# A planned instruction order: a short linger in TensorE's quarter form, and two constants of the order

## The chip, the cores and the metric

The kernel runs on one core of one Trainium2 chip. The metric is the device time of one execution in microseconds (us); lower is better. A core has TensorE (matmuls, results in eight banks of PSUM), VectorE (DVE in the profile), ScalarE (ACT), GpSimd (POOL) and SyncE (SP, which here only issues DMAs). Only VectorE and ScalarE copy results out of PSUM in this kernel.

## What is computed

Attention for 8 batches, 12 heads, 448 positions and 64 features a head, in which the heads are mixed before and after the softmax, and behind it a feed-forward layer on 3584 rows of 768:

```python
scores = scale * np.matmul(q, k.transpose(0, 1, 3, 2))
scores = np.einsum('bhij,hg->bgij', scores, w_pre)
scores = scores - np.max(scores, axis=-1, keepdims=True)
attn = np.exp(scores)
attn = attn / (np.sum(attn, axis=-1, keepdims=True) + 1e-09)
attn = np.einsum('bhij,hg->bgij', attn, w_post)
attn_out = np.matmul(attn, v)
x = attn_out.transpose(0, 2, 1, 3).reshape(B * S, H * D)
h = np.maximum(x @ w_in, 0.0)
out = h * h @ w_out
```

The matmuls work on bf16 data and sum in f32.

## The kernel before

**The work.** A batch is cut into 45 chunks of up to ten query positions by 12 heads (`chunk`, up to 120 rows and four rows of zeros), 360 chunks in all. Per batch and pair of heads, `score` multiplies q and k (L741) into a bank, and VectorE or ScalarE copies the bank to `snat` (`copy`, L534 and L536). `relayout` moves parts of `snat` by DMAs on SP's queue (L772) into one of 14 buffers `sch`, where the rows of a chunk are positions by heads. The mix of the heads is a matmul with `wmix`: for single chunks L901, for two chunks together `mix_two` (L847). Then follow the row minimum on VectorE (L912, the mix has the sign turned round), the exponential on ScalarE (L915), the reciprocal of the sums on VectorE (L922), the scaled weights `wq` on GpSimd (L925), four matmuls that turn the chunk and mix the heads again (L932), their copy to `atb`, and per half of a batch the product with v (`av`, L978). The feed-forward layer works in units of 128 or 256 rows (`unit`): L1037 multiplies by w_in, VectorE or ScalarE takes the positive part (L1051, L1055), GpSimd squares it (L1058), L1076 multiplies by w_out, and the result goes out through `osb`. These units fill the time in which the chunks leave TensorE free.

**Quarter form.** In the batches 1 to 7, most score groups and all of `mix_two` come as four 64x64 matmuls, each in a quarter of the TensorE array (`mode=BOTH` in the code, 3). This text calls such four a quarter group; one group fills two banks. `av` works in halves by columns (`COLS`), some scores of batch 0 in halves by rows (`ROWS`), all else on the whole array (mode 0, full form).

**The order.** All instructions are ordered in advance by a list scheduler in Python (`Planner`), and the engines then run their lists in order. An operation has a duration per engine (`engs`, ns), a delay until its result counts (`lat`), a priority (`pri`, in chunks; lower goes first), what it waits for, the PSUM banks that it takes (`bank`, a key whose first letter is the kind: m mixes, a turned chunks, g scores and others, f feed-forward) and the bank that it gives back (`frees`). `run` keeps a heap of ready operations for each engine, a list of free banks (`free`) and the room left for each kind (`room`, from `MOST`), and steps from event to event of its own clock. When TensorE is idle in that clock, it takes from the heap the first operation that `fits` (enough free banks and enough room), with these rules:

- If the operation is of another mode than the last one, it is set aside as `first`, and one of the same mode is looked for whose priority is at most `STAY[mode]` behind (2 chunks by rows, 6 by columns, 8 in quarter form; from full form there is no such rule).
- From another mode into quarter form it goes only if at least `TOGETHER` = 2 quarter groups would fit (`company`), or one is overdue (`due`).
- A change of mode is given 95 ns (`TURN`).
- An operation that doesn't fit is put into `kept`, and TensorE takes what fits, so it may leave quarter form for a full matmul while a quarter group waits for banks.

**Priorities and reserves that the change touches.** `score` and `relayout` subtract `AHEAD` (7.4 chunks) from the place of the chunk that they are for. From batch 2 on, `x_piece` turns k and q by DMA transposes on SP's queue (L673, L679). These need the heads side by side, which three "near copies" each of k and q on GpSimd make (`pair_k`, `pair_q`, L660, 640 ns in the order, of the lowest priority of all). The near copies wait in the order until `NEAR_LATE` = 3000 ns after the load of their data and after the previous transpose are done (`late`). This reserve is in the order alone; on the chip a copy waits for what it reads and for its turn in GpSimd's list.

Of the kernel before, what the change touches and what calls it, by code (L numbers as in the profile page):

```python
# [40 lines left out]
PIECE = NPAIR // 2  # L41
NE = 6
NSCH = 14
AHEAD = 7.4
FIFO = 50
IDLE_NS, IDLE_COLS, IDLE_FROM, IDLE_END, IDLE_LOW = 112, 256, 1300, 130000, 0.62
SPELL, PHASE, DROP, RISE = 3413, 1700, 0.4, 0.8
ROWS, COLS, BOTH = 1, 2, 3
PAIR_FROM, PAIRS, PAIR_MORE = 1, 1, 30
UP, ZERO_AT = 4, 4  # L50
TOGETHER, MIX_DUE, SCORE_DUE = 2, 1.5, 1.0
TURN = 95
LATER = 2
ONSET, ONSET_IDLE, ONSET_FROM = 2500, 2500, 20000
NEAR_LAST = 2e6
NEAR_LATE, NEAR_LATE_FROM = 3000, 2
OSTEP = 2
GS, ONE = [(0, 1, 2)], [(0,), (1,), (2,)]
STAY = {ROWS: 2, COLS: 6, BOTH: 8}
# [69 lines left out]
class Planner:  # L129
# [8 lines left out]
    def add(self, eng, ns, pri, fn, deps=(), lat=60, bank=None, frees=None, mode=0):  # L138
        op = Op(eng if isinstance(eng, dict) else {eng: ns}, lat, pri, fn, list(deps), bank, frees, mode)
        self.ops.append(op)  # L140
        return op
# [6 lines left out]
    def run(self):  # L148
        order, events, n = [], [], 0
        ready, busy, held = {}, {}, {}  # L150
        free, room = list(self.banks), dict(self.most)
# [13 lines left out]
        def fits(op):  # L165
            if not op.bank:
                return True
            kind, size = op.bank[0][0], len(op.bank)
            return len(free) >= size and room[kind] >= size and (room["mix"] >= size or kind == "f")

        t, mode, clock, front, turning = 0, 0, Clock(), -100, 0

        def company(heap):
            f, left, got = len(free), dict(room), 0
            for _, _, op in sorted(item for item in heap if item[2].mode == BOTH and item[2].eng is None):
                kind, size = op.bank[0][0], len(op.bank)
                if f >= size and left[kind] >= size and left["mix"] >= size:
                    f -= size
                    left[kind] -= size
                    left["mix"] -= size  # L180
                    got += 1
            return got
        queues = {"LOAD": Queue(), "DMA": Queue()}

        def settle():
# [13 lines left out]
        while True:  # L199
            for eng, heap in ready.items():  # L200
                if eng in queues:
                    x = queues[eng]
# [8 lines left out]
                    while x.op is None and heap:  # L211
                        op = heapq.heappop(heap)[2]
# [17 lines left out]
                if busy[eng] > t:  # L230
                    continue
                kept, short, first = [], False, None
                alone = eng == "PE" and mode != BOTH and company(heap) < TOGETHER
                while heap:
                    item = heapq.heappop(heap)
                    op = item[2]
# [17 lines left out]
                    if first is not None:  # L254
                        if op.mode != mode or op.pri > first[0] + STAY[mode]:
                            kept.append(item)
                            if op.pri > first[0] + STAY[mode]:
                                op, item = first[2], first
# [5 lines left out]
                else:  # L264
                    item = None
                    if first is not None:
                        kept.remove(first)
                        item, op, args = first, first[2], []
                if item is None and eng == "PE" and free and IDLE_FROM <= t < IDLE_END and (
                    t < 9000 or clock.at(t) > 1 or clock.share(t - SPELL, t) < IDLE_LOW  # L270
                ):
                    op = Op({"PE": 0}, 0, 0, self.still, [], None, None, mode)
                    op.eng, op.ns, op.at = "PE", IDLE_NS * clock.at(t), t
                    clock.spells.append((t, t + op.ns))
                    order.append((op, [free[0], mode]))
                    busy[eng] = t + op.ns
                    heapq.heappush(events, (t + op.ns, n, None))
                    n += 1
                if item is not None:
                    for key in op.bank:  # L280
                        held[key] = free.pop(0)
                        room[key[0]] -= 1
                        room["mix"] -= key[0] != "f"
                        args.append(held[key])
                    if len(op.engs) > 1:
                        args.append(eng)
                    op.eng, op.ns, op.at = eng, op.engs[eng], t
                    turning += op.turns
                    if op.front is not None:
                        front = op.front  # L290
                    if eng == "PE":
                        op.ns = (op.ns + TURN * (op.mode != mode)) * clock.at(t)
                        clock.spells.append((t, t + op.ns))
                        mode = op.mode
                    order.append((op, args))
                    busy[eng] = t + op.ns
                    heapq.heappush(events, (t + op.ns, n, None))
                    heapq.heappush(events, (t + op.ns + op.lat, n + 1, op))
                    n += 2
# [4 lines left out]
            t = events[0][0]  # L304
            while events and events[0][0] == t:
                op = heapq.heappop(events)[2]
                if op is None:
                    continue
                if isinstance(op, tuple) and isinstance(op[0], Queue):
                    x, turn_ = op  # L310
# [30 lines left out]
def kernel(  # L341
# [46 lines left out]
    def load_q(b, h0, h1):  # L388
        nc.gpsimd.dma_start(
            out=qs[:, h0:h1, :, :].rearrange("p h r d -> p h (r d)"),  # L390
            in_=q[b, h0:h1, 0:TAIL].rearrange("h (p r) d -> p h (r d)", r=NJ),
        )
# [6 lines left out]
    def load_kv(dst, src, b, h0, h1):  # L399
        nc.gpsimd.dma_start(  # L400
            out=dst[:, h0:h1, :, :].rearrange("p h r d -> p h (r d)"),
            in_=src[b, h0:h1].rearrange("h (p r) d -> p h (r d)", r=NB),
        )
# [143 lines left out]
    def load(rows, each, pri, fn, deps):  # L547
        if len(loads) >= 7:
            deps = list(deps) + [loads[-7]]
        op = add("POOL", 830, pri, fn, deps, lat=850)  # L550
        done = pl.moved("LOAD", rows, each[0], each[1], 0, [op], 1500)
        loads.append(done)
        return done
# [158 lines left out]
    def place_of(b, c):  # L712
        return b * NCHUNK + (ORDER0.index(c) if b == 0 else c)
# [6 lines left out]
    def is_direct(b, c):  # L720
        return b == 0 and C0[1] <= c <= C0[2]
# [5 lines left out]
    def score(b, r, group):  # L727
# [17 lines left out]
        first = min(place_of(b, c) for c in range(C0[r], (C0 + [NCHUNK])[r + 1]) if not is_direct(b, c)) - b * NCHUNK  # L745
        pri = b * NCHUNK + first - AHEAD - 0.6 - (0.7 if r == 0 else 1.4) * (NPAIR - p)
        n = b * (NJ + 1) + r - 2
# [30 lines left out]
    def relayout(b, c):  # L778
# [6 lines left out]
        deps = list(scopy[b, r]) + (list(scopy[b, r - 1]) if r == 1 and cc == 0 else [])  # L785
        pri = n - AHEAD
        if r == 2 and cc == 0:
# [15 lines left out]
        else:  # L803
            o = cc - 1
            if b >= PAIR_FROM:
                pri = n - o % (2 * PAIRS) + 0.1 * (o % (2 * PAIRS)) - AHEAD
            o, step = (2 * CI * (o // 2) + o % 2, 2) if b >= PAIR_FROM else (o, CPR)
# [324 lines left out]
    def gate(step):  # L1132
        return [wq_op[step]] if step in wq_op else []
# [62 lines left out]
    def load_tails(b, n, deps):  # L1196
        tails = [load(24, (24, 32), n, lambda x=x: load_tail(b, x), deps) for x in range(2)]
        tail_in[b] = add("TAIL", 0, n, lambda: None, tails, lat=1000 if b else 0)

    def load_ahead(b, n, g0):  # L1200
        wars = [op for p in range(g0 // 2, g0 // 2 + 3) for op in got_op[b - 1, p]]
        got = [
            load(48, (36, 52), n + LATER, lambda: load_q(b, g0, g0 + 6), wars + gate(n)),
            load(42, (46, 58), n + LATER, lambda: load_kv(ks, k, b, g0, g0 + 6), wars + gate(n)),
        ]
        if g0 == 0:
            load_tails(b, n + LATER, got_tail[b - 1] + gate(n))
        later[b, g0] = add("BOTH", 0, n, lambda: None, got, lat=0)
# [133 lines left out]
```

## Time and profile before

| what | value |
|---|---|
| median of 3 runs | 570.41 us (570.14 to 570.57) |
| the profiled execution | 569.92 us |
| its span, first to last instruction | 567.8 us |
| granted TensorE clock, mean | 1.0 |
| instructions | 17932 |
| quarter matmuls of `score`, L741 (64x64) | 504, mean 361 ns each |
| quarter matmuls of `mix_two`, L847 | 504, mean 363 ns each |
| copies to `snat`, VectorE / ScalarE | 150 of 613 ns / 168 of 551 ns |

The profile is one execution, taken by the hardware profiler. PE is TensorE's matmuls, PEld its weight loads, which overlap them. Matmuls are pipelined, so that the mean of one is longer than the distance to the next; the price of work on TensorE is read from the starts. "The chain of work that ended last" is followed back from the last instruction, at each step to what released it. "The waits" list idle time of an engine and what ended it. "The timeline" lists instructions by start, with like ones in a row merged: start, length, engine, line, operation, what is written and read, shapes, and a count behind an x.

### The profile page before, as it was taken

The page shows a single profiled execution, that of the slowest core. Times are in us where ns is not written, and L with a number is a line of the kernel's source. Part 1 is how long each engine was busy: PE and PEld are TensorE (multiplying, and loading weights), DVE is VectorE, ACT ScalarE, POOL GpSimd, SP SyncE. Part 2 cuts the span into 40 slices and gives each one's busy share as a digit, 9 for nine tenths or more (in the row PEclk, how much of TensorE's full clock was granted, in tenths as well). Part 3 has the DMA queues.
Part 4 walks back from the last instruction along what each step waited for, and adds up shares of the span by engine and source line. Part 5 has one row for each costly group of instructions (what it writes and reads, how often), then busy time and mean ns, then how long its engine had stood idle before and what let it go on. Part 6 is the DMA issues. An engine that isn't in the chain of part 4 may idle for free.

```text
span 567.8 us, 17932 instructions
## 1 busy us (share of the span) xinstructions
PE 559.7 (99%) x6323; PEld 396.5 (70%) x6323; DVE 496.8 (87%) x1108; ACT 447.9 (79%) x1187; POOL 363.7 (64%) x677
## 2 busy tenths in 40 slices
PE   8999999999999999999999999999999999999997
PEld 5668676686676667667677677767768676777785
DVE  7999999999999998999898988989899898898442
ACT  5788989888878888878998899888998988888100
POOL 8776358786685549856778358956777553745351
PEclk9999999999999999999999999999999999999999
DMA  9999849974999749974797649974798756441011
GB/s 137 211 178 217 165 117 181 208 135 103 151 203 153 175 97 181 176 162 101 136 198 161 161 104 162 195 145 128 131 192 164 134 142 108 111 99 58 1 57 55
DMA packets 129949, 80.85 MB, mean 142 GB/s; under 512 B 59274, under 2 KB 126588, under 8 KB 129860
## 3 DMA queue, kind: packets, MB, share of 16 engines
q1 hardware_dynamic: 80756, 46.29, 37.2%
q0 software_dynamic: 49104, 33.43, 36.3%
q8 instruction: 49, 0.80, 0.6%
q14 instruction: 40, 0.33, 0.1%
HBM read 45.61 MB, written 11.01 MB: 100 GB/s over the span
## 4 chain that ended last, share of the span: by engine, by line
PE 86%; DVE 5%; ACT 3%; issue 2%; POOL 2%; DMA 1%; DVEq 0%; ACTq 0%; POOLq 0%
PE bank L1076 25%; PE bank L1037 24%; PE bank L932 13%; PE bank L978 6%; PE bank L741 6%; PE bank L847 5%; PE bank L901 3%; DVE mn L912 2%; ACT es L915 2%; PE bank L907 1%; DMA sch<-snat 1%; PE bank L1301 1%; DVE atb L534 1%; PE bank L596 1%; POOL wq L925 1%
## 5 line engine op out<-in xcount | busy, mean ns | idle before, releaser
L915 ACT ACTIVATE es<-bank,mn 124x448 bf16<-124x448 f32 (+1 forms) x360 | 228.3, 643 | 34.3 <-DVE mn L912 30.0
L912 DVE TENSOR_REDUCE mn<-bank 124x1 f32<-124x448 f32 (+1 forms) x360 | 208.9, 612 | 6.8 <-PE bank L847 5.5
L1076 PE MATMUL bank<-w,h 128*128 128x384 bf16 (+2 forms) x912 | 180.2, 324 | 0.2 <-DVE hr L1051 0.2
L1037 PE MATMUL bank<-xt,w 128*128 128x256 bf16 (+1 forms) x1632 | 164.5, 254 | 0.7 <-ACT es L915 0.2
L1037 PEld LDWEIGHTS <-w 128*128 128x128 bf16 x1632 | 133.7, 98 | 25.3 <-issue 10.9
L1058 POOL TENSOR_TENSOR h<-hr 128x512 bf16<-128x512 f32 x112 | 115.9, 1038 | 40.3 <-DVE hr L1051 21.4
L925 POOL TENSOR_SCALAR wq<-wback_two,rc 124x120 bf16<-124x120 f32 x252 | 88.8, 363 | 72.0 <-DVE rc L922 49.2
L932 PEld LDWEIGHTS <-es 124*112 124x112 bf16 (+2 forms) x1440 | 107.0, 130 | 29.7 <-issue 4.9
L534 DVE CAST atb<-bank 112x480 bf16<-112x480 f32 (+3 forms) x196 | 118.1, 614 | 10.1 <-PE bank L932 8.9
L932 PE MATMUL bank<-wq,es 124*112 124x120 bf16 (+2 forms) x1440 | 119.1, 218 | 1.1 <-POOL wq L925 0.4
L1076 PEld LDWEIGHTS <-h 128*128 128x128 bf16 x912 | 79.6, 98 | 56.6 <-issue 18.1
L536 ACT CAST atb<-bank 112x480 bf16<-112x480 f32 (+3 forms) x187 | 99.2, 542 | 17.8 <-PE bank L932 16.6
L534 DVE CAST snat<-bank 128x448 bf16<-128x448 f32 x150 | 89.4, 613 | 3.3 <-PE bank L741 2.4
L536 ACT CAST snat<-bank 128x448 bf16<-128x448 f32 x168 | 85.0, 551 | 7.6 <-PE bank L741 6.8
L915 ACT ACTIVATION_READ_ACCUMULATOR es<-bank,mn 124x1 f32 (+1 forms) x360 | 75.3, 209 | 0.0
L1051 DVE TENSOR_SCALAR hr<-bank 128x512 f32<-128x512 f32 x76 | 52.2, 688 | 19.4 <-PE bank L1037 16.5
L925 POOL TENSOR_SCALAR wq<-wback,rc 124x120 bf16<-124x120 f32 (+1 forms) x94 | 33.4, 364 | 38.7 <-DVE rc L922 27.5
L741 PE MATMUL bank<-kt,qz 64*64 64x448 bf16 (+1 forms) x528 | 45.8, 361 | 0.7 <-ACT qz L536 0.6
L1100 POOL DMA_DIRECT2D out_dram<-osb x33 | 19.8, 600 | 35.5 <-DVE osb L534 18.1
L847 PE MATMUL bank<-sch,wmix 64*64 64x448 bf16 x504 | 42.4, 363 | 0.1
L978 PE MATMUL bank<-atb,vs 112*64 112x192 bf16 (+3 forms) x864 | 40.4, 250 | 0.0
L978 PEld LDWEIGHTS <-vs 112*64 112x64 bf16 x864 | 36.4, 110 | 3.9 <-issue 3.2
(80 smaller groups left out, 399.4 us busy)
## 6 DMA issues: line engine op xcount, KB each, us to landing
sch<-snat SPq DMA_DIRECT2D x318, 105.0 KB
out_dram<-osb POOLq DMA_DIRECT2D x21, 384.0 KB, 3.7
vs<-in_v_dram POOLq DMA_DIRECT2D x16, 336.0 KB, 7.4
ks<-in_k_dram POOLq DMA_DIRECT2D x14, 336.0 KB, 7.7
qs<-in_q_dram POOLq DMA_DIRECT2D x14, 288.0 KB, 7.1
w<-in_moe_w_in_dram POOLq DMA_DIRECT2D x6, 512.0 KB, 14.2
w<-in_moe_w_out_dram POOLq DMA_DIRECT2D x4, 768.0 KB, 20.6
out_dram<-osb POOLq DMA_DIRECT2D x8, 192.0 KB, 3.9
```

The source lines that it names most:

```text
L534: nc.vector.tensor_copy(out=out_, in_=in_)
L536: nc.scalar.copy(out=out_, in_=in_)
L741: nc.tensor.matmul(slot[m0:m1, 0:S], lhsT=lhsT[:, m0:m1], rhs=kt[i][half, :, at_, :], start=True, stop=True,)
L847: nc.tensor.matmul(got[i + x][o0:o1, 0:S], lhsT=w[k0:k1, c0:c0 + o1 - o0], rhs=srcs[i + y][k0:k1, :], start=True, stop=True,)
L912: nc.vector.tensor_reduce(out=mn[i][0:rows, :], in_=slots[mk][0:rows, 0:S], axis=AX.X, op=ALU.min)
L915: nc.scalar.activation(out=es[i][0:rows, 0:S], in_=slots[mk][0:rows, 0:S], func=ACT.Exp, scale=-1.0, bias=mn[i][0:rows, 0:1], accum_out=sm ...
L925: nc.gpsimd.tensor_scalar(out=wq[i][0:rows, :, 0:ns], in0=back[0:rows, :, 0:ns], scalar1=rc[i // 2][0:rows, i % 2:i % 2 + 1], scalar2=1.0, ...
L932: nc.tensor.matmul(slot[0:P_KEYS, jb * H * ns:(jb + 1) * H * ns], lhsT=es[i][0:rows, jb * P_KEYS:(jb + 1) * P_KEYS], rhs=wq[i][0:rows, :, ...
L978: nc.tensor.matmul(v_[64 * hh:64 * hh + 64, i, 0:x1 - x0], lhsT=vs[:, 2 * c2 + hh, jb, :], rhs=atb[half][:, jb, 2 * c2 + hh, x0:x1], start ...
L1037: nc.tensor.matmul(slot[:, j * w:(j + 1) * w], lhsT=w1[c2][:, (f0 + j) * 128:(f0 + j + 1) * 128], rhs=xt[:, c2, a:z], start=(c2 == 0), sto ...
L1058: nc.gpsimd.tensor_tensor(out=h2_[:, f0:f0 + nf, 0:w], in0=hr[gi % 2][:, :].rearrange("p (f c) -> p f c", f=nf), in1=hr[gi % 2][:, :].rear ...
L1076: nc.tensor.matmul(slot[:, 0:c1 - c0], lhsT=h2_[:, ft, mt * 128:(mt + 1) * 128], rhs=w2[:, ft, c0:c1], start=(ft == 0), stop=(ft == FT - 1),)
```

## The change

A new function `soon` looks at the quarter groups that are ready but don't fit, takes the first by priority, and goes through the copies out of PSUM that are under way and end within `LINGER` = 120 ns in the order's clock. If these free enough banks and room for that group, it gives the time at which they do. Where TensorE is about to go from quarter form to an operation of another mode, the order asks `soon`. If there is such a time, the operation is put back, nothing is issued, and TensorE looks again at that time. Besides, `AHEAD` goes from 7.4 to 7.5 chunks, and `NEAR_LATE` from 3000 to 2000 ns. No instruction is added or removed except by the order (the fillers on `still`, L1301, are placed by it up to 130 us); the same matmuls, copies and DMAs run in another sequence.

```diff
--- before.py
+++ after.py
@@ -41,7 +41,7 @@
 PIECE = NPAIR // 2
 NE = 6
 NSCH = 14
-AHEAD = 7.4
+AHEAD = 7.5
 FIFO = 50
 IDLE_NS, IDLE_COLS, IDLE_FROM, IDLE_END, IDLE_LOW = 112, 256, 1300, 130000, 0.62
 SPELL, PHASE, DROP, RISE = 3413, 1700, 0.4, 0.8
@@ -50,10 +50,11 @@
 UP, ZERO_AT = 4, 4
 TOGETHER, MIX_DUE, SCORE_DUE = 2, 1.5, 1.0
 TURN = 95
+LINGER = 120
 LATER = 2
 ONSET, ONSET_IDLE, ONSET_FROM = 2500, 2500, 20000
 NEAR_LAST = 2e6
-NEAR_LATE, NEAR_LATE_FROM = 3000, 2
+NEAR_LATE, NEAR_LATE_FROM = 2000, 2
 OSTEP = 2
 GS, ONE = [(0, 1, 2)], [(0,), (1,), (2,)]
 STAY = {ROWS: 2, COLS: 6, BOTH: 8}
@@ -180,6 +181,20 @@
                     left["mix"] -= size
                     got += 1
             return got
+
+        def soon(kept):
+            waiting = sorted(x for x in kept if x[2].mode == BOTH and not fits(x[2]))
+            if not waiting:
+                return None
+            op = waiting[0][2]
+            kind, size = op.bank[0][0], len(op.bank)
+            f, k, mix = len(free), room[kind], room["mix"]
+            for at, _, x in sorted(e for e in events if e[0] <= t + LINGER and isinstance(e[2], Op) and e[2].frees is not None):
+                f, k, mix = f + 1, k + (x.frees[0] == kind), mix + (x.frees[0] != "f")
+                if f >= size and k >= size and mix >= size:
+                    return at
+            return None
+
         queues = {"LOAD": Queue(), "DMA": Queue()}
 
         def settle():
@@ -276,6 +291,13 @@
                     busy[eng] = t + op.ns
                     heapq.heappush(events, (t + op.ns, n, None))
                     n += 1
+                if item is not None and eng == "PE" and mode == BOTH and op.mode != mode:
+                    at = soon(kept)
+                    if at is not None:
+                        kept.append(item)
+                        item = None
+                        heapq.heappush(events, (at, n, None))
+                        n += 1
                 if item is not None:
                     for key in op.bank:
                         held[key] = free.pop(0)
```

## The prediction

> **What bounds the kernel now.** I read the page's busy times first, then its chain of work that ended last.
>
> ```profile
> PE 559.7 (99%) x6323; PEld 396.5 (70%) x6323; DVE 496.8 (87%) x1108; ACT 447.9 (79%) x1187; POOL 363.7 (64%) x677
> ...
> PE 86%; DVE 5%; ACT 3%; issue 2%; POOL 2%; DMA 1%; DVEq 0%; ACTq 0%; POOLq 0%
> ```
>
> TensorE is busy for 99% of the span and carries 86% of the chain, so the time is about the sum of its instructions. A busy PE is not a PE without gaps (its ends are modelled), so I next took the waits, TensorE's alone, and then a table by stretches.
>
> ```profile
> PE bank L1301 <- DVE still L406: 1.1, 1, 1.1
> PE bank L901 <- DVE atb L534: 0.6, 1, 0.6
> ```
>
> ```profile
> 100.00:200.00 100.00, 99.18 (x1155) 69.99 (x1151) 95.09 (x207) 83.51 (x224) 68.53 (x132) 1.00 0.81 161
> 200.00:300.00 100.00, 99.71 (x1104) 70.06 (x1101) 91.50 (x199) 85.53 (x226) 69.91 (x129) 1.00 0.82 151
> 300.00:400.00 100.00, 99.88 (x1146) 71.03 (x1145) 91.58 (x199) 86.83 (x232) 66.56 (x127) 1.00 0.74 149
> ```
>
> The longest waits of TensorE are 1.1 and 0.6 us, once each. In the stretches (columns: length, then PE, PEld, DVE, ACT, POOL busy, granted clock, DMA share, GB/s) the clock is 1.00 and VectorE is 92 to 95% busy, so it has little slack behind TensorE. Only a smaller sum of TensorE's own work, or of its hidden losses, can move the end. One such loss is in the timeline of TensorE:
>
> ```profile
> 280.40 0.38 PE L741 MATMUL bank<-kt,qz 64*64 64x448 bf16 x4
> 280.72 0.50 PE L1076 MATMUL bank<-w,h 128*128 128x384 bf16 x2
> 281.15 0.38 PE L741 MATMUL bank<-kt,qz 64*64 64x448 bf16 x4
> 281.36 0.36 PE L847 MATMUL bank<-sch,wmix 64*64 64x448 bf16 x4
> 281.65 0.50 PE L1076 MATMUL bank<-w,h 128*128 128x384 bf16 x2
> 281.99 0.59 PE L932 MATMUL bank<-wq,es 124*112 124x120 bf16 x8
> ```
>
> Only the first column (starts) is needed. A quarter group (four 64x64 matmuls) that another follows takes 0.21 us (281.15 to 281.36); one that a full matmul follows takes 0.32 or 0.29. Two output matmuls (L1076) take 0.34 us before a full matmul, 0.43 before a quarter one. So each change of form costs some 0.09 us. At 280.72 TensorE left quarter form for two matmuls and came back.
>
> **The price of a return trip.** I took the distance from each start to the next over the whole timeline. Medians: L1076 to L1076 163 ns, to a quarter group 256, so entering costs 93 (L932: 52 and 145, again 93). Quarter group to one of the other kind 203, to L1076 284, so leaving costs 81. A return trip costs 174 ns. The 252 quarter groups stand in 129 runs (30 of one group, 75 of two, 24 of three), so there are 128 trips, 22.3 us in all: the most that this change could ever win.
>
> **How often the new rule acts.** It acts where a run ends, a quarter group waits for banks alone, and a copy that frees enough ends within 120 ns. I counted the state of the eight banks from the trace at each of the 128 exits (a bank is taken by its first matmul and free at the end of its copy out; the exit is put 81 ns before the next start). At 44 exits the banks for the next quarter group were already free, so data or priorities ended the run and nothing changes. At 15 the release came within 120 ns, at 69 later. With 70 ns more for a semaphore it is 11. I take 13. The short trips are mostly not among them: 12 of the 128 take under 0.8 us as the one at 280.72 does, and at 11 of these the banks were already free.
>
> **The sum.** Each saves 174 ns and costs the wait, between 0 and 120 ns, on average 60: 13 x (174 - 60) = 1.5 us. That counts one trip for each wait: a group that is pulled forward ends a trip if it was alone in its run, or if the rest is pulled along. If the runs only grow, 13 of 252 groups no longer need a place, and 13 / 1.95 (groups to a run) = 6.7 trips go: 1.2 - 0.8 = 0.4 us. With no wait at all it is 13 x 174 = 2.3 us. The term lies between -0.4 and -2.3; no row decides between them, so I take the middle, -1.4.
>
> While TensorE waits, what is queued behind it are the full matmuls that it would have run. Nobody is short of them: GpSimd and VectorE feed L1076 and L1037 ahead of time (by the waits, TensorE stands for hr 0.4 us in the whole run).
>
> **AHEAD 7.4 to 7.5** moves the priority of every score group and relayout a tenth of a chunk forward, 0.16 us at 567.8 / 360. Score groups, their copies on VectorE and ScalarE and the moves on SP's queue all move past one another by that much. The waits that this could shorten, for sch from DMA, are 2.5 us in all (TensorE and its weight loads), and a tenth of a chunk reaches little of them. It also redraws the order from the first microseconds on. By the distances between starts, TensorE began late for something 56 times, 9.5 us in all, 4.7 of them in the first 100 us. I set the redraw at nothing, with half of these 4.7 on either side: -2.3 to +2.3.
>
> **NEAR_LATE 3000 to 2000** lets the near copies of batches 2 to 7 come up to 1 us sooner.
>
> ```profile
> L660 POOL COPY kn<-ks x36: 599/609/624, 106.5 to 438.6; 112x512 bf16<-112x512 bf16 x36
> L660 POOL COPY qn<-qs x36: 497/502/507, 108.1 to 445.9; 128x384 bf16<-128x384 bf16 x36
> its engine sat idle before it (us, times) until:
> ```
>
> Nothing stands under the last line: no copy ever waited for its load. From landing to the first copy the trace has 4.0 us at least (landed 414.29, copied 418.32), so with 1 us less 3 us remain and GpSimd does not block. The transposes on SP's queue follow sooner. Behind a copy on GpSimd stand wq (363 ns) and the squares; a wq that comes 0.6 us later has cover, since by the waits TensorE stands for wq 0.4 us in all. If that cover went in two places it would cost 2 x 0.6 = 1.2 us; what could be gained is the waits for transposed data, under 0.4 us after the first batch. I take 0.
>
> So the profiled execution (569.92 us: span 567.8 and 2.1 around it) would come to 568.5. The median of the runs is 570.41, 0.5 above it, so I forecast **569.0 us**.
>
> **Rivals.**
> *More trips go (0.13).* If waiting once brings the next group too, the 30 runs of one group go: 30 x (174 - 60) = 3.4 us, 567.0. For it: copies that free a bank come some 1270 times in 568 us, one each 0.45 us. Against: 69 of 128 exits are further from a release than 120 ns.
> *It does next to nothing (0.22).* Groups move from one run to the next, trips stay: -0.4 to 0, 570.2. For it: 99 of the 129 runs hold two or three groups, so a group pulled out leaves its run standing, and the short trips are out of its reach. Against: a wait of 120 ns at most costs less than the 174 of a trip.
> *It stalls (0.22), slower.* Now the quarter groups come long after their banks are free: by the trace a median of 1.03 us, and only 5 of 504 banks under 150 ns. The new order puts a group right behind a copy. If VectorE or ScalarE is one instruction behind there, TensorE, which works in order, waits for a whole copy (snat 613 on VectorE, 551 on ScalarE), some 0.6 us, with full matmuls ready behind it. If 6 of 13 are late: 6 x 0.6 + 7 x 0.06 - 13 x 0.174 = +1.8, 572.2. It decides from a mean wait of 174 ns, or some 3 late of 13. For it: VectorE at 92% and more. Against: TensorE's late starts between 100 and 500 us are only 31, 4.3 us.
> The Trainium skill (TensorEngine Tiling (Array Packing), PSUM Bottleneck) speaks for this rival: packing makes TensorE faster but not the copies out of PSUM, which may become the limit. By that rule the change is worth nothing or less, and the time that of this rival; VectorE's 87% and TensorE's 99% do not bear it out as yet.
> *The clock falls (0.01).* The filler of the first 10 us (128x256, L1301) starts 213 ns apart, the same shape in L1037 later 108, so TensorE does run at half speed at the start. 10 us of that again would cost 5 us, 575. Against: the granted clock stays 1.00 from 183 to 187 us, with the longest late start (0.75 us at 184.1); 120 ns are less.
> The Trainium skill (TensorE: Matmul & The Clock Gate, A second HAM failure mode: psum-queue depth-cycling) warns of short idle times between groups that make the clock go up and down; no row here shows it after the start.
>
> **Chances.** The forecast has 0.42. A measurement of this kernel can tell about 0.2% from no change, 1.14 us: faster is under 569.27, slower over 571.55. Of the forecast 0.06 lies above 569.27 if the wins are few; of "next to nothing" the redraw throws 0.03 to either side. Faster: 0.36 + 0.13 + 0.03 = 0.52. Same: 0.06 + 0.16 = 0.22. Slower: 0.22 + 0.01 + 0.03 = 0.26. The range takes in the term's -2.3 with most of the fusing rival, and most of the stall rival: 566.7 to 571.9; outside it are the ends of the redraw, the worst stalls and the clock.
>
> **What would show it.** In the changed profile, 7 to 13 fewer quarter runs in TensorE's timeline, fewer runs of one group; 174 ns a trip unchanged; TensorE's busy sum about 1.4 us smaller; waits in front of L741 and L847 of 0.1 us, not 0.6; no wait before L660. It is wrong if the runs are as many as before, if late starts grow by more than 1.5 us, or if the end moves with the first 100 us, where no quarter run stands before 81 us.

## The result, and the profile after

| | before | after |
|---|---|---|
| median of 21 runs each, us | 570.28 (569.25 to 571.57) | 569.03 (567.59 to 570.45) |
| ratio, 95% interval | 1 | 0.9979 (0.9971 to 0.9987) |
| the profiled execution, us | 569.92 | 569.35 |
| quarter runs / changes of form in TensorE's timeline | 129 / 311 | 125 / 306 |

The change saves 1.2 us, 0.21%; 569.0 was forecast. The two profiled executions stand only 0.6 us apart, since the one of before lies 0.4 below its median and the one of after 0.3 above.

Part of the gain lies outside what the profile shows. A run's device time holds more than the span from the first to the last instruction: 2.05 to 2.17 us more in the 73 runs of before that were timed beside the experiments, 1.72 to 1.84 in the 21 of after. So some 0.35 of the 1.2 us lie outside the span, where no matmul and no copy stands, and about 0.9 inside. What the 0.35 are isn't shown; e1, e2, e3, e5 and e9 below have the shorter time outside too, e4, e6, e7 and e8 the longer one, so that it doesn't follow any one of the three edits.

The page of the changed kernel, its busy times and its chain:

```profile
PE 558.4 (98%) x6323; PEld 397.4 (70%) x6323; DVE 500.7 (88%) x1112; ACT 446.9 (79%) x1183; POOL 363.4 (64%) x677
...
PE 89%; DMA 3%; POOL 2%; DVE 2%; ACT 2%; issue 1%; ACTq 0%; POOLq 0%; DVEq 0%; SPq 0%
```

TensorE is busy for 1.3 us less with the same 6323 matmuls, and has more of the chain. Its waits, and the same stretches as before (length, then PE, PEld, DVE, ACT, POOL busy, granted clock, DMA share, GB/s):

```profile
PE bank L618 <- DMA qs<-in_q_dram: 1.0, 2, 0.5
PE bank L646 <- DVE qz L556: 0.8, 1, 0.8
PE bank L869 <- DMA sch<-snat: 0.4, 2, 0.2
```

```profile
100.00:200.00 100.00, 99.34 (x1148) 70.14 (x1145) 91.60 (x198) 80.30 (x218) 68.84 (x132) 1.00 0.80 154
200.00:300.00 100.00, 99.31 (x1091) 68.76 (x1088) 94.62 (x204) 88.52 (x232) 67.86 (x128) 1.00 0.81 154
300.00:400.00 100.00, 99.88 (x1143) 72.39 (x1141) 89.88 (x194) 82.53 (x218) 67.16 (x124) 1.00 0.72 149
```

The first two waits lie ahead of 14 us, with the first loads (L618 and L646 are L596 and L624 of before), and come and go between executions: a kernel with the order of before there (e6 below) showed them too. The longest single wait is the 1.1 us at the very start, as in before, and the clock stays at 1.00.

**A way to split the time.** For each kind of step of TensorE and what comes next I took the median distance between starts over the profiled executions of all the kernels below. The sum of these medians is the normal time of an order; it grows with the changes of form. What an execution takes beyond it are its late starts (less the early ones).

| kernel (one profiled execution) | quarter runs | changes of form | normal time, us | late starts, net, us | first to last start, us |
|---|---|---|---|---|---|
| before | 129 | 311 | 549.0 | 14.4 | 563.4 |
| after | 125 | 306 | 548.4 | 14.8 | 563.1 |
| e1 linger alone | 130 | 314 | 549.2 | 21.6 | 570.8 |
| e2 both constants alone | 136 | 327 | 550.4 | 17.9 | 568.2 |
| e3 AHEAD alone | 141 | 338 | 551.6 | 13.2 | 564.8 |
| e4 NEAR_LATE alone | 136 | 326 | 550.5 | 17.0 | 567.5 |
| e5 after, pulls undone | 139 | 333 | 550.7 | 14.8 | 565.5 |
| e9 linger and AHEAD | 127 | 310 | 548.7 | 21.5 | 570.3 |
| e10 linger and NEAR_LATE | 127 | 308 | 548.7 | 16.7 | 565.4 |
| e11 after, NEAR_LATE 500 | 127 | 310 | 548.8 | 12.1 | 560.9 |

From 311 to 338 changes the normal time grows by 2.6 us, 96 ns each, near the 87 of half a trip. Between these ten orders the normal time moves by 3.2 us, the late starts by 9.5.

Two cautions. The 9.5 us of late starts in the prediction and the expectations count only single starts that are clearly late, in before; the 14.4 here are the sum of all differences. And each row is one execution: those of e1, e4 and e9 took 1.8 to 2.4 us more than the medians of their kernels and that of e3 0.9 less, while the others lie within 0.6, so that as much of the late starts in these rows is the execution's and not the order's.

### The profile page after: what moved, and what is told of

Same layout as the page of the kernel before. It is cut to its first block, busy times and chain, and to the rows that moved or that the text cites. A ratio compares the mean times of both kernels' runs of the same rounds, so it can differ in the third digit from the quotient of the medians.

```text
span 567.6 us, 17890 instructions
## 1 busy us (share of the span) xinstructions
PE 558.4 (98%) x6323; PEld 397.4 (70%) x6323; DVE 500.7 (88%) x1112; ACT 446.9 (79%) x1183; POOL 363.4 (64%) x677
## 4 chain that ended last, share of the span: by engine, by line
PE 89%; DMA 3%; POOL 2%; DVE 2%; ACT 2%; issue 1%; ACTq 0%; POOLq 0%; DVEq 0%; SPq 0%
PE bank L1098 26%; PE bank L1059 25%; PE bank L954 14%; PE bank L1000 7%; PE bank L763 7%; PE bank L869 5%; PE bank L923 3%; DMA sch<-snat 2%; PE bank L929 1%; DMA qs<-in_q_dram 1%; ACT es L937 1%; POOL wq L947 1%; PE bank L618 1%; DVE osb L912 1%; DVE hr L1073 0%
## 5 line engine op out<-in xcount | busy, mean ns | idle before, releaser
L1098 PE MATMUL bank<-w,h 128*128 128x384 bf16 (+2 forms) x912 | 179.7, 323 | 0.1
L954 PEld LDWEIGHTS <-es 124*112 124x112 bf16 (+2 forms) x1440 | 107.9, 129 | 30.9 <-issue 5.6
L556 DVE CAST atb<-bank 112x480 bf16<-112x480 f32 (+3 forms) x195 | 116.7, 608 | 9.6 <-PE bank L954 8.8
L954 PE MATMUL bank<-wq,es 124*112 124x120 bf16 (+2 forms) x1440 | 120.5, 217 | 1.0 <-POOL wq L947 0.4
L558 ACT CAST atb<-bank 112x480 bf16<-112x480 f32 (+3 forms) x188 | 101.0, 548 | 22.3 <-PE bank L954 20.6
L1098 PEld LDWEIGHTS <-h 128*128 128x128 bf16 x912 | 79.8, 98 | 53.4 <-issue 14.7
L556 DVE CAST snat<-bank 128x448 bf16<-128x448 f32 x149 | 87.7, 614 | 1.7 <-PE bank L763 0.6
L1073 DVE TENSOR_SCALAR hr<-bank 128x512 f32<-128x512 f32 x83 | 57.1, 688 | 19.3 <-PE bank L1059 15.3
L763 PE MATMUL bank<-kt,qz 64*64 64x448 bf16 (+1 forms) x528 | 45.8, 362 | 0.1
L869 PE MATMUL bank<-sch,wmix 64*64 64x448 bf16 x504 | 42.7, 361 | 0.4 <-DMA sch<-snat 0.4
```

The lines of the kernel that those rows point to most:

```text
L556: nc.vector.tensor_copy(out=out_, in_=in_)
L558: nc.scalar.copy(out=out_, in_=in_)
L763: nc.tensor.matmul(slot[m0:m1, 0:S], lhsT=lhsT[:, m0:m1], rhs=kt[i][half, :, at_, :], start=True, stop=True,)
L869: nc.tensor.matmul(got[i + x][o0:o1, 0:S], lhsT=w[k0:k1, c0:c0 + o1 - o0], rhs=srcs[i + y][k0:k1, :], start=True, stop=True,)
L954: nc.tensor.matmul(slot[0:P_KEYS, jb * H * ns:(jb + 1) * H * ns], lhsT=es[i][0:rows, jb * P_KEYS:(jb + 1) * P_KEYS], rhs=wq[i][0:rows, :, ...
L1098: nc.tensor.matmul(slot[:, 0:c1 - c0], lhsT=h2_[:, ft, mt * 128:(mt + 1) * 128], rhs=w2[:, ft, c0:c1], start=(ft == 0), stop=(ft == FT - 1),)
```

## The experiments

Two questions: does the linger bring the gain (theory A), or do the three edits merely draw another order whose late starts happen to be few (theory B)? Ratios are against the kernel before, run on the same chip.

### One edit, or two, at a time: e1 to e4

e1 is the changed kernel with the two constants of before:

```diff
-AHEAD = 7.5
+AHEAD = 7.4
-NEAR_LATE, NEAR_LATE_FROM = 2000, 2
+NEAR_LATE, NEAR_LATE_FROM = 3000, 2
```

> soon and LINGER = 120 alone; AHEAD 7.4 and NEAR_LATE 3000 as before. Its order has 130 quarter runs (before 129, after 125). Theory A, the linger itself brings the gain by fewer trips of 174 ns: with no trip fewer here it should be within 0.5 us of before, 569.8 to 570.8, TensorE's late starts as before (9.5 us). Theory B, each of the three edits draws a new order of the whole kernel, and the draw is worth more than the trips: the time lies several us from before in spite of one run more or less, 572 to 576, and the difference stands in late starts of TensorE, not in trips.

574.61 us, ratio 1.0069 (1.0050 to 1.0087).

e2 is the changed kernel without the linger:

```diff
-LINGER = 120
+LINGER = -1
```

> AHEAD 7.5 and NEAR_LATE 2000 as after, no linger (LINGER = -1, so that soon never finds anything). Its order has 136 quarter runs against 125 of after. Theory A: 11 trips more than after, 11 x (174 - 60) = 1.3 us slower than after, 570.3, late starts as after. Theory B: the order is another draw, so the time differs from after by more than the trips can, 572 to 576, most of it late starts.

574.24 us, 1.0065 (1.0047 to 1.0083).

e3 is the kernel before with one constant:

```diff
-AHEAD = 7.4
+AHEAD = 7.5
```

> AHEAD 7.5 alone, on the kernel before. Its order has 141 quarter runs against 129. Theory A (trips are what counts): 12 x 0.174 = 2.1 us slower than before, 572.4. Theory B (the draw counts): off from before by up to some 5 us either way and not by the trips; late starts differ from 9.5 us by more than 2 us.

571.88 us, 1.0028 (1.0014 to 1.0043).

e4 is the kernel before with the other:

```diff
-NEAR_LATE, NEAR_LATE_FROM = 3000, 2
+NEAR_LATE, NEAR_LATE_FROM = 2000, 2
```

> NEAR_LATE 2000 alone, on the kernel before. Its order has 136 quarter runs against 129. Theory A: 7 x 0.174 = 1.2 us slower than before, 571.5, and no copy on GpSimd waits for its load (at least 3 us between landing and copy). Theory B: off by the draw, 568 to 575, with late starts that make up the difference.

572.12 us, 1.0035 (1.0014 to 1.0056).

Each edit alone makes the kernel slower, and so do the two constants together. e3 is what theory A said (571.88 for 572.4): 27 more changes of form, no more late starts. e4 has some of both, and both theories' numbers hold it; no near copy waits in it, with 2.8 us at least between landing and copy (3 were expected). e1 and e2 are theory B's: e1 has but three changes of form more than before, yet 7.2 us more late starts (some 5 when the slow execution is allowed for). TensorE's waits in e1:

```profile
PE bank L923 <- DMA sch<-snat: 1.6, 1, 1.6
PE bank L618 <- DMA qs<-in_q_dram: 1.2, 2, 0.7
PE bank L763 <- DMA kt<-kn: 1.2, 1, 1.2
```

Two single waits for DMAs on SP's queue, a relayout (at 119 us) and a transpose (at 193 us), are 2.8 us of it; TensorE stands until they land. Nothing of the kind is in before.

### The linger in a fixed order: e5

Here nothing is drawn anew. Behind the planner, 14 groups that a linger had pulled forward go back behind the full matmul that they had passed:

```diff
+        for late, soon_ in swaps:
+            place = {id(e[0]): x for x, e in enumerate(order)}
+            order.insert(place[id(soon_)], order.pop(place[id(late)]))
         return order
```

> The changed kernel's own order, with 14 of its lingers undone behind the planner: wherever TensorE had lingered and then taken a quarter group, the full matmul that had been put off (where it takes no new bank) goes ahead of that group again. All else keeps its place, so no new order is drawn. 139 quarter runs instead of 125. Theory A (a linger saves a trip of 174 ns and waits little, some 35 ns in the order's clock): 14 x (174 - 35) = 1.9 us slower than after, 571.0, with late starts as after. Theory C (the lingers wait for copies that come late, so that the trips saved are paid back): within 0.5 us of after, 568.6 to 569.5, with late starts smaller by some 2 us.

571.50 us, 1.0022 (1.0008 to 1.0036). Against after (0.9979) that is 0.43% or 2.4 us (1.5 to 3.4 by the two intervals), theory A: 0.17 us for each pull (0.11 to 0.24), the price of a trip with little or nothing off for the wait. The split agrees: 27 changes of form more, normal time up by 2.3 us, late starts 14.8 in both. One place in the timeline of TensorE, first in after, then in e5 (L763 and L775 are L741 of before, L869 and L881 L847, L1098 and L1110 L1076, L954 and L966 L932):

```profile
171.89 0.57 PE L763 MATMUL bank<-kt,qz 64*64 64x448 bf16 x8
172.40 0.82 PE L1098 MATMUL bank<-w,h 128*128 128x384 bf16 x4
173.15 0.38 PE L869 MATMUL bank<-sch,wmix 64*64 64x448 bf16 x4
173.36 0.53 PE L763 MATMUL bank<-kt,qz 64*64 64x448 bf16 x4
173.82 0.50 PE L1098 MATMUL bank<-w,h 128*128 128x384 bf16 x2
174.16 0.58 PE L954 MATMUL bank<-wq,es 124*112 124x120 bf16 x8
```

```profile
172.43 0.38 PE L775 MATMUL bank<-kt,qz 64*64 64x448 bf16 x4
172.75 0.50 PE L1110 MATMUL bank<-w,h 128*128 128x384 bf16 x2
173.18 0.38 PE L775 MATMUL bank<-kt,qz 64*64 64x448 bf16 x4
173.49 0.50 PE L1110 MATMUL bank<-w,h 128*128 128x384 bf16 x2
173.92 0.38 PE L881 MATMUL bank<-sch,wmix 64*64 64x448 bf16 x4
174.23 0.50 PE L1110 MATMUL bank<-w,h 128*128 128x384 bf16 x2
174.66 0.38 PE L775 MATMUL bank<-kt,qz 64*64 64x448 bf16 x4
174.98 0.63 PE L966 MATMUL bank<-wq,es 124*112 124x120 bf16 x8
```

Both do four quarter groups and six output matmuls before the L932 of before (L954, L966). After needs 2.27 us in two runs (171.89 to 174.16), e5 2.55 in four. The wait can be seen too: the second group of the run, at 173.36, takes 0.46 us to the next start, where 0.29 is the median. VectorE's copy out of its second bank ended at 173.46, and the matmuls into that bank start at 173.52. So 0.17 us went into the wait and 0.28 were gained: the two trips were worth 0.45 us, more than 2 x 0.174.

The timelines of before, after and e5 show most of why. From the start of a quarter group to what follows it takes 213 ns if that is another quarter group, 292 if the group ends a run of two or three, and 315 if it is alone in its run. So leaving costs 79 ns after a longer run, which the prediction's 81 is, and 102 after a lone group. A pull takes away lone groups (51 runs of one in e5, 25 in after), and the trip of a lone group costs 93 + 102 = 195 ns.

### The price of a trip by itself: e6 and e7

An extra matmul on zeros goes ahead of every quarter group, in full form in e6 and in quarter form in e7, into a bank that the group then overwrites:

```diff
+    def touch(slot):
+        k_, m_ = (P, P) if 0 == 0 else (P // 2, P // 2)
+        nc.tensor.matmul(
+            slot[0:m_, 0:64], lhsT=still[0:k_, 0:m_], rhs=still[0:k_, 0:64], start=True, stop=True,
+        )
...
+            touch(got[0])
```

> The kernel before with an extra matmul on zeros of 64 columns in FULL form ahead of each of the 252 quarter groups, into the bank that the group then overwrites. 123 groups that followed another one in quarter form now have a trip before them. Theory A (a trip costs 174 ns, none of it hidden): slower than the twin with the extra matmul in quarter form by 123 x 0.174 = 21 us, give or take 4 for the extra matmuls themselves. Rival (the price by the starts is partly hidden): under 10 us.

> The twin: the same extra matmul of 64 columns in QUARTER form, so that no trip is added. Each takes at most the 51 ns that a quarter matmul of 448 columns has on average: 0 to 13 us slower than before, 570 to 583, with 129 quarter runs.

e6 600.11, e7 573.78 us: 26.3 us apart, at most 214 ns for each of 123 added trips. Part of that is the extra matmul in full form. Where it adds no trip it costs 29 ns (two L1076 and then a quarter group start 448 ns apart in e6, 419 in before); the one in quarter form costs 16 by e7's time (3.9 us over 252). By these two numbers 252 x 13 ns = 3.3 us are the matmul itself, and an estimate of some 0.19 us is left for a trip, here always that of a lone group. So the price by the starts is borne out and nothing of it is hidden.

### The missing draws and two others: e8 to e12

All are the changed kernel with other constants. e8:

```diff
-AHEAD = 7.5
+AHEAD = 8.1
-LINGER = 120
+LINGER = 60
-NEAR_LATE, NEAR_LATE_FROM = 2000, 2
+NEAR_LATE, NEAR_LATE_FROM = 2500, 2
```

> The changed kernel with AHEAD 8.1, NEAR_LATE 2500 and LINGER 60: another draw of the order, in which TensorE is done 1.9 us sooner than in after by the order's own clock, with 122 quarter runs against 125. Theory A (trips alone): 3 x 0.174 = 0.5 us faster than after, 568.5. Theory B (the draw counts, and the order's clock shows most of it): 567.2, within 1.5 us. Nothing gained from the draw (the order's clock is no guide to 2 us): 569 to 572.

569.93 us, 1.0000 (0.9980 to 1.0020): nothing gained from the draw. Its order has the fewest changes of form of all, 297, and its late starts (16.1 us) take that back.

e9:

```diff
-NEAR_LATE, NEAR_LATE_FROM = 2000, 2
+NEAR_LATE, NEAR_LATE_FROM = 3000, 2
```

> Linger 120 and AHEAD 7.5, NEAR_LATE still 3000: one of the two draws that are missing from the eight that three edits on or off can give. Its order has 127 quarter runs, before 129. Theory A (trips decide): 2 x 0.174 = 0.3 us faster than before, 569.6. Theory B (the draw decides): TensorE is done 6.5 us later than before by the order's own clock; that clock has so far been off by up to 2 us against the chip, so 574 to 579, with late starts up by some 5 us.

574.63 us, 1.0075 (1.0050 to 1.0100), theory B. Nearly all of its additional late starts stand in one place, from 160 to 173 us, and not all of them are waits: from 167 to 174 us the granted clock was 0.50 (last section). TensorE was busy for 5.2 us there, so that by an estimate 2.6 us are the clock's. All five runs have a mean clock under 1 (0.994 to 0.997).

e10:

```diff
-AHEAD = 7.5
+AHEAD = 7.4
```

> Linger 120 and NEAR_LATE 2000, AHEAD still 7.4: the other missing draw. 127 quarter runs. Theory A: 569.6. Theory B: 1.4 us later than before by the order's own clock, so 569 to 573.5. If the linger as such is worth something, the four pairs with and without it must on average favour it.

571.29 us, 1.0015 (0.9998 to 1.0032); theory B's range holds it, theory A's 0.3 us faster than before (0.9994) lies just below the interval.

With these the eight combinations are complete. What the linger does, in each pair with equal constants: +0.69% (7.4, 3000: e1 against before), +0.47% (7.5, 3000: e9, e3), -0.20% (7.4, 2000: e10, e4), -0.86% (7.5, 2000: after, e2). The mean is +0.03%, with a standard deviation of 0.7%: four draws can't show whether a linger pays on average in a redrawn order. The expectation that they would favour it failed.

e11:

```diff
-NEAR_LATE, NEAR_LATE_FROM = 2000, 2
+NEAR_LATE, NEAR_LATE_FROM = 500, 2
```

> The changed kernel with NEAR_LATE 500 instead of 2000: near copies up to 1.5 us sooner again, 127 quarter runs against 125. Theory A: 2 x 0.174 slower than after, 569.4. Theory B: 1.2 us sooner than after by the order's own clock, 567.9, within 2 us. Theory D (a reserve this small lets GpSimd stand for loads that land late): copies at L660 wait, 570 or more.

567.60 us, 0.9954 (0.9936 to 0.9972), theory B's number, and **faster than both kernels**. Its late starts are the fewest, 12.1 us; it has two quarter runs more than after. Whether it is fast because it is another draw, or because transposed data come sooner, this run doesn't separate. Its near copies, in the view of their line:

```profile
L682 POOL COPY kn<-ks x36: 599/612/623, 103.4 to 436.8; 112x512 bf16<-112x512 bf16 x36
L682 POOL COPY qn<-qs x36: 493/508/518, 106.9 to 442.2; 128x384 bf16<-128x384 bf16 x36
...
its engine sat idle before it (us, times) until:
  DMA kt<-kn: 2.0, 1
```

One copy waited 2.0 us, not for its load but for the transpose that had to leave `kn`. From landing to copy there are still 1.4 us at least (after: 3.8). So GpSimd did stand once, though not for theory D's reason, and it costs too little to show.

e12:

```diff
-AHEAD = 7.5
+AHEAD = 7.8
```

> The changed kernel with AHEAD 7.8: a draw with 130 quarter runs against 125, yet TensorE done 1.0 us sooner by the order's own clock. Theory A: 5 x 0.174 = 0.9 us slower than after, 569.9. Theory B: 568.0, within 2 us, with late starts smaller than in after.

575.71 us, 1.0065 (1.0034 to 1.0096); both theories missed it, by some 6 us (the medians stand 0.9% apart; its runs are spread so far that the two figures differ). Two views of its profile, TensorE's waits and a table by stretches:

```profile
PE bank L763 <- ACT snat L558: 4.7, 1, 4.7
```

```profile
133.90:137.30 3.40, 0.00 (x0) 0.00 (x0) 0.00 (x0) 0.00 (x0) 0.00 (x0) 1.00 0.56 162
137.30:144.10 6.80, 5.68 (x37) 3.43 (x37) 4.46 (x10) 3.92 (x9) 4.22 (x7) 0.50 0.32 78
```

Relayout DMAs landed late; the copies to `snat` waited 6 us for them, TensorE 4.7 us for the copies, and after 3.4 us without any work the granted clock was 0.50 for 6.8 us. Why the DMAs were late isn't shown. Its ten runs lie from 570.06 to 577.55; the six with a mean clock of 0.990 to 0.994 took 575 and over, and one at 0.997 took 575.68.

**What the order's own clock knew.** Each kernel's `Planner` also says when TensorE is done in its clock. Beside it, the medians on the chip; both are differences to before in us, on the same chip:

| | after | e1 | e2 | e3 | e4 | e8 | e9 | e10 | e11 | e12 |
|---|---|---|---|---|---|---|---|---|---|---|
| the order's clock | +0.3 | +4.4 | +4.5 | +3.2 | +2.5 | -1.6 | +6.5 | +1.4 | -0.9 | -0.7 |
| measured | -1.3 | +4.6 | +4.3 | +1.9 | +2.2 | +0.1 | +4.3 | +1.0 | -2.7 | +5.4 |

Nine of ten agree within 2.2 us: that clock had each edit alone, and the two constants together, slower than before. It can't tell kernels apart that differ by less than some 2 us, and it doesn't know e12's late DMAs.

## Why the forecast was right, and where only its sum was

- **The price of a trip, 174 ns**: right. 0.17 us for each pull in e5, after its wait, and some 0.19 in e6 and e7. It is the price behind longer runs; that of a lone group is 195.
- **How often the rule acts, 13**: low. 21 groups were pulled in the changed order, 14 of them past a matmul that takes no bank, which e5 undoes; the runs that went, 11 against e2, lie within the 7 to 13. The 70 ns for a semaphore came from no row; in before's ten waits of TensorE on another engine it starts 53 ns (median) after the end of what it waited for.
- **The wait, 60 ns each**: too dear. In the order's clock the 21 lingers last 37 ns on average, and on the chip the late starts are the same with and without 14 of them (14.8 us). The stall rival (572.2) did not happen; nor did the clock fall in the changed kernel.
- **The term, -1.4 for trips**: this step failed as put, though the total came out. It took the trips of before as those that would stand without the rule. With the new constants and no linger there are 136 runs, not 129 (e2); the linger takes away 11 and leaves 125. "7 to 13 fewer" was right against e2 and wrong against before, where it is 4, or 0.7 us.
- **The redraw, 0 within 2.3**: failed in size. By e2 the constants alone cost 3.7 us by the ratio (0.65%), outside the bounds; the linger then gives 4.9 us back (0.86%). By e5 some 2.4 of these are 14 of its 21 pulls in the given order. The other 2.5 us are the remaining 7 pulls and the draw again, not separated: which late starts an order has, changes with each edit. Two terms that were off by more than the forecast gain cancelled, and that the total came out within 0.1 us of the forecast is luck. The bounds came from half of the late starts of the first 100 us; e1's came at 119 and 193 us, from DMAs.
- **The time around the span, 2.1 us**: taken as fixed, it fell by some 0.35 us, for a reason that isn't shown.
- **NEAR_LATE, 0 for waits on GpSimd**: right for after. No copy waits there, and 3.8 us are left between landing and copy (4.0 before). In e2, with the same constants, one copy waits 2.0 us for a transpose, as in e11. What the edit does stands in the redraw.
- **The short trips out of reach**: wrong. Trips under 0.8 us are 12 in before, 17 in e2 and 9 in after, and with 14 pulls undone (e5) they are 23: such trips are what the linger takes away, as at 172.75, 173.49 and 174.23 above. The count at the exits of before could not show it, for the rule acts in another order.
- **What stays open**: which part of the 0.9 us inside the span is trips (0.7 by four runs) and which the draw, beyond the single profiled executions; these differ by 0.6 us, and runs of one kernel move by about 1 us.

The Trainium skill (TensorEngine Tiling (Array Packing), PSUM Bottleneck) says that once matmuls are packed, the copies out of PSUM may become the limit. In e5 this does not decide, since 14 groups put right behind copies cost no late starts with VectorE at 88%.

## What to carry to other kernels

Judge a new ordering rule in a fixed order, by undoing its effects one for one behind the planner, for a change of constants moves the time by more than the rule. When a rule comes with re-tuned constants, count with the constants alone as the base, for which the planner has to run and no chip is needed: here it gave 136 quarter runs and 4.5 us more, and the chip 4.3. Set the range by what other draws cost: here from -0.5% to +0.8%. Late starts decide between draws, single late DMAs on a shared queue among them (e1, e12). The planner's own clock shows what a draw costs to some 2 us, but it had nothing of e12's late DMAs.

## What the runs showed of the hardware

In e12 the granted clock fell to 0.50 for 6.8 us, 3.6 us into TensorE's wait of 4.7 us. In e9 it fell without so long a gap: in the stretches before, TensorE was busy for 2.53 of 3.42 us and then 1.89 of 3.42, and no single wait was over 1.4 us there:

```profile
160.36:163.78 3.42, 2.53 (x28) 2.02 (x28) 2.02 (x4) 2.05 (x7) 2.19 (x4) 1.00 1.43 197
163.78:167.20 3.42, 1.89 (x16) 0.61 (x13) 2.74 (x8) 1.60 (x5) 2.37 (x6) 1.00 1.40 215
167.20:174.00 6.80, 5.17 (x36) 3.91 (x40) 4.18 (x9) 4.64 (x12) 4.51 (x9) 0.50 0.85 160
```

The Trainium skill (TensorE: Matmul & The Clock Gate, What's actually happening) puts the half clock after an idle window of some 3.4 us. e12 agrees (3.4 us without work, then 0.50); e9 shows that a window which is busy for 55% by the profile can do it too. Two more such stretches, each followed by the next, from e10 and from e1:

```profile
7.42:10.83 3.41, 1.47 (x35) 0.93 (x34) 3.20 (x11) 2.19 (x5) 3.41 (x6) 1.00 1.46 161
10.83:14.25 3.42, 3.42 (x36) 1.85 (x35) 3.32 (x12) 2.72 (x7) 3.14 (x6) 0.50 1.55 182
```

```profile
117.65:121.07 3.42, 1.78 (x22) 1.38 (x21) 2.79 (x6) 1.10 (x3) 3.28 (x6) 1.00 0.62 125
121.07:124.48 3.41, 3.41 (x35) 2.94 (x34) 2.24 (x5) 3.04 (x9) 1.70 (x4) 1.00 0.49 134
```

In e10 the clock fell after TensorE was busy for 43%, in e1 it stayed after 52%. With the traces of this case cut in this way, in step with their changes of the clock, no stretch that was busy for 62% or more is followed by a fall, and between 52 and 56% both occur. The busy share is the profile's, whose ends of matmuls are modelled, so these figures are no sharp limit.
